# Transposing a tile's attention output with one DMA of 512 columns in place of four of 128

## The chip, the cores and the metric

One core of a Trainium2 chip (trn2). The metric is the device time of one execution in microseconds (us). The profiler's span is some 1.8 to 2.0 us shorter than that time, because it runs from the first to the last instruction alone. Each execution carries a state; all timed runs used here are of state fast. Single looks (the one profiled run, whose state is unknown) are marked as such. Three words recur. A DMA's landing is the moment when all its data have arrived. A hold is the time by which an instruction starts late because it waits for such a landing. The granted clock is the share of full speed at which TensorE was allowed to run.

## The reference, cut to what matters

Attention over 4 batches, 8 heads, 768 positions and head size 64 (three heads with the full causal mask, five with four sink positions and a window of 64), then a gated feed-forward layer on the result:

```python
scores = where(mask, q @ k.T / sqrt(64), -1e9)
attn_out = softmax(scores) @ v                                  # 4 x 8 x 768 x 64
x = attn_out.transpose(0, 2, 1, 3).reshape(3072, 512)           # a row: all 8 heads of one position
g = x @ w_gate                                                  # 512 x 1536
out = (g * sigmoid(g) * (x @ w_val)) @ w_out                    # 1536 x 512
```

## The kernel before

The 3072 rows are 24 tiles of 128. Four tiles make a group: group 3 is tiles 12 to 15, group 4 is 16 to 19, group 5 is 20 to 23. The attention of a tile ends in `xb`, 128 rows by 512 columns in fp16. The feed-forward matmuls contract over those 512 columns, so they need them on the partitions: `xt`, four blocks of 128 columns each, transposed. The order of all tasks on all engines is fixed in a list in the kernel, so no engine picks other work while it waits.

```python
def norm(t, odd):                        # VectorE: writes half of xb
    if t not in xbs:
        xbs[t] = buf("xb", [128, 4, 2, 64], FH, "xb")          # ring of 3
    ...

def xtranspose(t):
    xb = xbs.pop(t)
    g, n = GROUP[t]
    if g not in xts:
        xts[g] = buf("xt", [128, 4, 512], FH, "xt")            # ring of 2
    if t >= XBAR:                        # XBAR = 12: the later twelve tiles, by DMA
        for p in range(4):
            nc.sync.dma_start_transpose(
                out=xts[g][:, p, n * 128:(n + 1) * 128],
                in_=xb[:, p].rearrange("p a d -> p (a d)"))
        return
    tr = buf("tr", [128, 4, 128], FH, "xtr")                   # the first twelve, by TensorE
    for p in range(4):
        nc.tensor.transpose(tr[:, p, :], xb[:, p].rearrange("p a d -> p (a d)"), ident)
    trs[t] = tr

def xevac(t):                            # VectorE: the first twelve tiles alone
    g, n = GROUP[t]
    nc.vector.tensor_copy(out=xts[g][:, :, n * 128:(n + 1) * 128], in_=trs.pop(t))

def gate(g, j, c, wsb, d):               # the first reader of xt
    ps = d[g, j, c] = buf("gv", [128, 512], FP, "gv")[:, 0:c[1] - c[0]]
    for kk in range(4):
        nc.tensor.matmul(ps, wsb[:, kk, j * 128:(j + 1) * 128], xts[g][:, kk, c[0]:c[1]],
                         start=(kk == 0), stop=(kk == 3))

def store(g, tt):                        # on the same sync queue as the transposes
    ...
    for j in range(2):
        eng = nc.scalar if j and final else nc.sync
        eng.dma_start(out=rows[j], in_=o_sb[j * 64:(j + 1) * 64, :])
```

The sync engine's queue (SP) issues, in the list's order, all loads, all transposes by DMA, and the stores. An issue that has to wait holds up everything behind it (from_4_to_10 below shows a load issued 7.7 us later for that).

The softmax here doesn't subtract the row's maximum and nothing guards it: scores larger than these inputs give would overflow.

## Time and profile before

| | before |
|---|---|
| time, median of 3 runs | 271.9 us (271.53 to 271.96) |
| span of the profiled run | 269.9 us |
| TensorE busy over the span; from 128 to 227 us | 96%; 99.00 of 99.00 us |
| transposes by DMA | 48, first issue at 129.3 us, last at 222.9 us |
| share of the 16 DMA engines, 128 to 227 us | 0.20 |

How to read it: the share over the span mixes a start in which loads and casts set the pace with a long stretch in which TensorE has no gap. The transposes by DMA all lie in that stretch.

### The profile page before, as it was taken

Reading aid. Unit: us, or ns where it says so; the run is one execution under the profiler, and the core shown is the slowest. Engines: PE = TensorE matmul, PEld = TensorE weight load, DVE = VectorE, ACT = ScalarE, POOL = GpSimd, SP = SyncE. Lnnn points to the kernel's source line nnn. Section 1 sums busy time; section 2 is a strip of 40 time slices with the busy share of each in tenths; the row PEclk is TensorE's granted clock in tenths of the full one; section 3 lists DMA queues with packets and bytes.
Section 4 is the critical chain, followed back from the end, with each engine's and each line's share of the span. In section 5 each row is a group of like instructions: output and inputs, shape, how many; then the busy total and the mean of one; then the engine's idle time right before and its main releaser. Section 6 shows DMA issues by size and latency. Waiting matters only on the chain.

```text
span 269.9 us, 5396 instructions
## 1 busy us (share of the span) xinstructions
PE 258.0 (96%) x2063; PEld 150.4 (56%) x2063; DVE 173.6 (64%) x340; ACT 167.0 (62%) x260; POOL 113.1 (42%) x145
## 2 busy tenths in 40 slices
PE   7799889899999999999999999999999999999993
PEld 7777546465655565465556655555555544444441
DVE  6757787896679487657668257764582565555321
ACT  2499779999897568777657964495564603141300
POOL 6669936774786541875523223366320200000000
PEclk9999999999999999999999999999999999999998
DMA  7999999999940999011012411202002312110144
GB/s 191 294 347 350 332 282 357 341 290 294 288 150 14 257 311 275 3 40 41 19 27 58 92 40 26 56 19 62 1 15 61 89 24 51 39 40 0 41 102 92
DMA packets 56954, 36.53 MB, mean 135 GB/s; under 512 B 9312, under 2 KB 52320, under 8 KB 56928
## 3 DMA queue, kind: packets, MB, share of 16 engines
q1 hardware_dynamic: 56848, 36.06, 50.4%
q8 instruction: 16, 0.26, 0.4%
q10 hardware_dynamic: 80, 0.13, 0.2%
q14 instruction: 10, 0.08, 0.1%
HBM read 28.31 MB, written 6.29 MB: 128 GB/s over the span
## 4 chain that ended last, share of the span: by engine, by line
PE 80%; ACT 12%; DVE 5%; issue 2%; ACTq 0%
PE gv L762 42%; PE o_ps L791 21%; PE sc L524 9%; PE av L557 5%; ACT e L540 4%; PE tr L413 3%; ACT v L178 2%; ACT hq L178 2%; ACT sig L768 1%; ACT vt L178 1%; DVE m L264 1%; PE xtr L583 1%; DVE v L290 1%; DVE k L289 1%; DVE wg_sb L180 1%
## 5 line engine op out<-in xcount | busy, mean ns | idle before, releaser
L540 ACT ACTIVATE e<-sc 128x1024 f16<-128x1024 f32 (+4 forms) x67 | 60.9, 909 | 22.9 <-PE sc L524 22.5
L762 PE MATMUL gv<-xt,wg_sb 128*128 128x512 f16 (+1 forms) x304 | 71.9, 368 | 1.7 <-DVE wg_sb L180 1.1
L762 PE MATMUL gv<-xt,wv_sb 128*128 128x512 f16 (+1 forms) x304 | 72.3, 368 | 0.0
L548 POOL TENSOR_TENSOR e<-e,m 128x640 f16<-128x640 f16 (+1 forms) x25 | 44.5, 1787 | 65.8 <-ACT e L540 65.7
L791 PE MATMUL o_ps<-wo_sb,h 128*128 128x512 f16 x288 | 71.8, 379 | 0.3 <-ACT o_sb L178 0.3
L768 ACT ACTIVATE sig<-gv 128x512 f32<-128x512 f32 (+1 forms) x76 | 43.1, 575 | 44.7 <-PE gv L762 42.9
L772 DVE SCALAR_TENSOR_TENSOR sil<-sig,gv 128x512 f32<-128x512 f32 (+1 forms) x76 | 49.5, 656 | 31.8 <-ACT sig L768 31.2
L779 DVE SCALAR_TENSOR_TENSOR h<-sil,gv 128x512 f16<-128x512 f32 (+1 forms) x76 | 48.8, 654 | 9.6 <-PE gv L762 8.5
L762 PEld LDWEIGHTS <-wg_sb 128*128 128x128 f16 x304 | 28.9, 98 | 29.3 <-DVE wg_sb L180 1.4
L762 PEld LDWEIGHTS <-wv_sb 128*128 128x128 f16 x304 | 28.8, 98 | 26.5 <-issue 0.2
L791 PEld LDWEIGHTS <-h 128*128 128x128 f16 x288 | 26.6, 98 | 26.4 <-issue 0.7
L524 PE MATMUL sc<-qT,kT 128*128 128x256 f16 (+1 forms) x228 | 35.2, 257 | 1.4 <-ACT e L540 0.8
L180 POOL COPY v<-vt 32x528 f16<-32x528 f16 (+1 forms) x46 | 29.4, 640 | 6.4 <-ACT vt L178 3.7
L524 PEld LDWEIGHTS <-kT 128*128 128x128 f16 x228 | 20.6, 98 | 13.3 <-issue 2.7
L180 POOL CAST vt<-raw 64x512 f16<-64x512 f32 x30 | 18.7, 625 | 16.2 <-DMA raw<-in_v_dram 11.3
L557 PEld LDWEIGHTS <-e 128*128 128x128 f16 x472 | 20.1, 97 | 7.5 <-issue 0.5
L565 DVE RECIPROCAL rc<-av 128x4 f32<-128x4 f32 x48 | 8.6, 180 | 24.1 <-PE av L557 23.7
L178 ACT CAST hq<-raw 128x512 f16<-128x512 f32 x32 | 19.3, 617 | 4.2 <-DMA raw<-in_q_dram 2.9
L557 PE MATMUL av<-vt,e 128*128 128x65 f16 x392 | 21.7, 193 | 0.2 <-DVE xb L566 0.2
L566 DVE TENSOR_TENSOR xb<-av,rc 128x256 f16<-128x256 f32 x48 | 20.4, 424 | 1.7
L413 PE MATMUL tr<-ident,hq 128*128 128x128 f16 x192 | 15.0, 219 | 2.1 <-DVE m L264 1.1
L413 PEld LDWEIGHTS <-hq 128*128 128x128 f16 x192 | 12.2, 98 | 5.6 <-DVE m L264 1.2
(57 smaller groups left out, 192.1 us busy)
## 6 DMA issues: line engine op xcount, KB each, us to landing
raw<-in_q_dram SPq DMA_DIRECT2D x12, 512.0 KB, 7.2
raw<-in_k_dram SPq DMA_DIRECT2D x12, 512.0 KB, 7.0
raw<-in_v_dram SPq DMA_DIRECT2D x12, 512.0 KB, 7.5
out_dram<-o_sb SPq DMA_DIRECT2D x47, 128.0 KB, 2.3
raw<-in_moe_w_gate_dram SPq DMA_DIRECT2D x6, 512.0 KB, 8.7
raw<-in_moe_w_val_dram SPq DMA_DIRECT2D x6, 512.0 KB, 8.7
raw<-in_moe_w_out_dram SPq DMA_DIRECT2D x6, 512.0 KB, 7.6
xt<-xb SPq DMA_TRANSPOSE x48, 2.3
```

The source lines that it names most:

```text
L178: nc.scalar.copy(out=dst, in_=src)
L180: ENG[task.way[0]].tensor_copy(out=dst, in_=src)
L413: nc.tensor.transpose(tr[:, p, :, j, :] if w else tr[:, j, p, :], hqs[n][:, w, j, p // 2, (p % 2) * 128:(p % 2 + 1) * 128], ident)
L524: nc.tensor.matmul(sc[c // 4][:, c % 4:c % 4 + n, :], weights, moving, start=first, stop=last)
L540: nc.scalar.activation(out=e[:, 0:n], in_=whole_sc.pop((t, u))[:, 0:n], func=AF.Exp, scale=scale)
L548: ENG[task().way[0]].tensor_tensor(out=ev, in0=ev, in1=mm, op=ALU.mult)
L557: nc.tensor.matmul(av[:, n, 0:65], ee, vv, start=(m == 0), stop=(m == len(bl) - 1))
L762: nc.tensor.matmul(ps, wsb[:, kk, j * 128:(j + 1) * 128], xt[:, kk, c[0]:c[1]], start=(kk == 0), stop=(kk == 3))
L768: nc.scalar.activation(out=sg[g, j, c], in_=gs[g, j, c], func=AF.Tanh, scale=0.5)
L772: nc.vector.scalar_tensor_tensor(out=sl[g, j, c], in0=sg.pop((g, j, c)), scalar=1.0, op0=ALU.add, in1=gs.pop((g, j, c)), op1=ALU.mult)
L779: nc.vector.scalar_tensor_tensor(out=hs[g, j][:, c[0]:c[1]], in0=sl.pop((g, j, c)), scalar=0.5, op0=ALU.mult, in1=vs.pop((g, j, c)), op1=A ...
L791: nc.tensor.matmul(o_open[g, tt], hs[g, j][:, tt * 128:(tt + 1) * 128], wo_sb[:, j, :], start=(j == 0), stop=(j == NJ - 1))
```

## The change

The intent: one instruction for a tile in place of four. It saves 36 of 48 issues on the sync queue and should bring each tile's transposed block sooner.

```diff
         if t >= XBAR:
-            for p in range(4):
-                nc.sync.dma_start_transpose(
-                    out=xts[g][:, p, n * 128:(n + 1) * 128],
-                    in_=xb[:, p].rearrange("p a d -> p (a d)"))
+            nc.sync.dma_start_transpose(
+                out=xts[g][:, :, n * 128:(n + 1) * 128],
+                in_=xb.rearrange("p a b d -> p (a b d)"))
             return
```

## The prediction

> **What bounds the kernel now.** I read four views, in this order: the engines' shares and the chain of waits on the profile's page, busy time by stretch, the waits of TensorE, and then the timeline of the queue that issues the transposes (SP, the sync engine) beside TensorE's.
>
> The page first:
>
> ```profile
> PE 258.0 (96%) x2063; PEld 150.4 (56%) x2063; DVE 173.6 (64%) x340; ACT 167.0 (62%) x260; POOL 113.1 (42%) x145
> PE 80%; ACT 12%; DVE 5%; issue 2%; ACTq 0%
> xt<-xb SPq DMA_TRANSPOSE x48, 2.3
> ```
>
> TensorE is busy for 258.0 of 269.9 us, and 80% of the chain that ended last is TensorE. No DMA is among the engines of that chain. The last line is what the change touches: 48 transposes, four for each of tiles 12 to 23, each landing a median 2.3 us after its issue.
>
> An average hides stages, so next the busy time by stretch (columns: stretch, length, TensorE busy with its matmul count, granted clock, mean share of the 16 DMA engines, GB/s):
>
> ```profile
> 0.00:70.00 70.00, 62.76 (x678) 1.00 1.09 307
> 70.00:128.00 58.00, 58.00 (x457) 1.00 0.57 148
> 128.00:227.00 99.00, 99.00 (x755) 1.00 0.20 44
> 227.00:270.00 43.00, 38.26 (x178) 0.97 0.21 49
> ```
>
> The idle of TensorE lies before 70 us, where loads, casts and masks set the pace, and in the last few microseconds. The transposes run from 129.3 us (the first starts there) to about 226 us. In just that stretch TensorE is busy for 99.00 of 99.00 us at full clock, and the DMA engines are at 0.20.
>
> Busy time is modelled from pipelined matmuls, so I did not stop there. The waits of TensorE over the whole run name warm-up, masks, weight casts, exps and evictions, the largest 1.4 us; none is a DMA. Restricted to 120 to 265 us the list is empty. Short holds can be too small for that list, so I looked at the three places where TensorE first needs a group's transposed activations. Tiles 12-23 form groups 3, 4 and 5 of four tiles each; the first gate matmul of group 3 is number 161 of the 304 that read wg_sb (64 of group 0, then 48 for each group), of group 4 number 209, of group 5 number 257. Those stand at 151.83, 187.87 and 225.26 us:
>
> ```profile
> 151.83 1.11 PE L762 MATMUL gv<-xt,wg_sb 128*128 128x512 f16 x4
> 155.80 1.89 PE L762 MATMUL gv<-xt,wg_sb 128*128 128x512 f16 x8
> 187.87 1.03 PE L762 MATMUL gv<-xt,wg_sb 128*128 128x512 f16 x4
> 225.26 2.01 PE L762 MATMUL gv<-xt,wg_sb 128*128 128x512 f16 x8
> ```
>
> And the last four transposes of each group on the queue (start, time from first to last issue):
>
> ```profile
> 146.34 5.02 SPq L577 DMA_TRANSPOSE xt<-xb  x4
> 181.24 4.92 SPq L577 DMA_TRANSPOSE xt<-xb  x4
> 219.09 5.00 SPq L577 DMA_TRANSPOSE xt<-xb  x4
> ```
>
> The reader sees how tight the schedule is. Group 3's fourth transpose is issued at 150.13 and lands 2.4 us later, at 152.5, while its first gate matmul starts at 151.83: it already runs, because the first of its four matmuls needs only the first of the four 128-column pieces. Group 4's last lands at 187.3 (184.93 + 2.4), 0.55 us ahead of 187.87. Group 5's last lands at 225.9 (222.85 + 3.1), behind 225.26. So two starts should show a hold, and they do: four matmuls take 1.11 us in place of 1.03 (the undisturbed four at 187.87), eight take 2.01 in place of 1.89 (the undisturbed eight at 155.80). The holds are 0.08 and 0.12 us. **That is all the time that TensorE gives to these transposes: 0.20 us.**
>
> **What the Trainium skill says.** "VectorE: DVE Perf Modes", section "The three transpose paths", gives 1309 ns for a 128x128 transpose through the DMA crossbar. The trace's issue on the queue has a median of 1.23 us (48 instructions), near that; to landing it is 2.3 us. "DMA: Bandwidth & Descriptors", section "Rules for kernel authors", says to join many small transfers into a large one, since under 64 KB one pays mostly overhead. The trace agrees: one piece is 32 KB (128 x 128 x 2 B), and over 130 to 145 us, with only transposes in flight, the share of the DMA engines is 0.12, so a transpose keeps them busy for about 0.15 us (0.12 x 15 us / 12) out of 2.3. The same page, section "Latency and other measured facts", has 261 GB/s for DMA transposes that are not contiguous; 32 KB at that rate is 0.13 us, and my 0.15 fits. "Perfetto Trace Analysis", section "Optimization Strategies", says to optimize what the matmul engine waits for when it idles; here it doesn't idle, so that advice doesn't point at the transposes.
>
> **The change, part by part.**
> - Removed: 36 of 48 issues on the SP queue. Four back to back take 5.0 us.
> - Added: the remaining 12 are four times as large, 128 KB. If the overhead is per instruction, the issue stays near 1.2 to 1.7 us, and landing is 2.3 + 3 x 0.15 = about 2.8 us. Both are estimates from the numbers above. The queue is freed by about 12 x (5.0 - 1.5) = 42 us; nothing but stores follows on it in this stretch.
> - Moved: a tile's transposed block is complete about 2.8 us after the first issue in place of 6.2 (146.34 to 152.5), some 3.4 us earlier. For the first matmul of a group the wait becomes one for the whole block in place of one piece after another, but the block would be there at about 149.1, 184.0 and 221.9 us, ahead of 151.83, 187.87 and 225.26 by 2.7 to 3.9 us.
> - Moved: stores issued behind transposes go out up to 3.5 us sooner, so output buffers come free sooner.
> - Unchanged: TensorE's instructions and their order (fixed in a list), the first 129 us, and the end, where TensorE works through the last output products and the final eviction and store follow.
>
> Sum on the path: minus 0.08 minus 0.12 us; the other 42 us lie beside TensorE's work. An earlier store relieves no hold that TensorE shows in this stretch, so it counts as 0. 271.9 - 0.2 = **271.7 us**.
>
> **The rivals.**
> 1. The latency of the transposes is on the path. Then 3.4 us would come off at each group boundary, 10 us in all, and the time would be about 261.7. For it: landing and use lie within a microsecond of each other at all three boundaries. Against it, decisively: the matmuls start on time but for 0.20 us, other matmuls having been placed ahead of them.
> 2. The wide transpose costs the same as four (cost per 128 columns, not per instruction). Then the block lands when the fourth piece did, but the first matmul waits for all of it: group 3 starts at 152.5 in place of 151.83, group 5 at 225.9 in place of 225.26, some 0.7 us each where 0.2 in all was lost: about +1.2, so 273.1 us. If even the landing time of 2.3 us scaled by four (9.2 us), the three starts would slip to 155.5, 190.4 and 228.3, by 3.7, 2.5 and 3.0 us: about 281 us, 3.3% slower. Against it: the engines are busy for 0.15 us of 2.3, and most of the rest should not grow with size. What no line shows is how this chip handles a source of four column groups in one instruction.
> 3. The sooner stores free output buffers and help the evictions. For it: VectorE waits 2.1 us once for a store to land. Against it: TensorE's waits on evictions after 120 us are none, so at most a tenth or two, inside the range.
>
> **Range and chances.** The change's own effect is 0 to -0.2 us in the main case, up to +1.2 in the milder form of rival 2, which I give one in ten. The three runs before spread over 0.43 us. I choose 271.1 to 272.4: the predicted value with that spread on both sides, a little more above for rival 2. Faster by over 2% would need 5.4 us and TensorE has no such idle time in the stretch: 0.01. Slower by over 2% needs the strong form of rival 2 or something unseen: 0.02. Within 2%: 0.97.
>
> **What would show each step right or wrong.** Right: 12 transposes, each issued in under 2 us and landing in under 3.5; TensorE busy in all of 128 to 227 us; first gate matmuls of the three groups at nearly the same times with four in 1.03 and eight in 1.89; fewer waits in the SP queue behind transposes and earlier stores. Rival 2: issue of about 5 us each, landing in 6 or more, and a TensorE wait on xt at one of the boundaries. Rival 1: the chain from 128 us on shorter by microseconds. The prediction is wrong if the time leaves 271.1 to 272.4, above all if TensorE's matmuls between 128 and 227 us move by more than half a microsecond.

## The result, and the profile after

The changed kernel is correct. Its median is 271.43 us (271.0 to 271.52, 4 runs), against 271.74 us (271.53 to 271.96, 4 runs) of the kernel before. The ratio is 0.9985, with a 95% interval of 0.9968 to 1.0003: the same at 2%, and even no difference at all lies inside. (A ratio is the mean time of one kernel's fast runs over that of the other's in the same rounds, so not quite the ratio of the medians quoted.)

The page of the kernel after: the engines' shares, the chain by engine, and the row of the transposes (count, median us from issue to landing).

```profile
PE 257.9 (96%) x2063; PEld 150.2 (56%) x2063; DVE 173.6 (64%) x340; ACT 167.1 (62%) x260; POOL 113.0 (42%) x145
PE 80%; ACT 12%; DVE 5%; issue 2%; ACTq 0%
xt<-xb SPq DMA_TRANSPOSE x12, 2.4
```

Four times the data, and 2.4 us to landing where it was 2.3. The engines' busy times and the chain are what they were. The queue in the timeline of the kernel after (start, time from first to last issue, count):

```profile
129.31 12.32 SPq L576 DMA_TRANSPOSE xt<-xb  x3
...
143.66 1.20 SPq L576 DMA_TRANSPOSE xt<-xb  x1
...
181.21 1.19 SPq L576 DMA_TRANSPOSE xt<-xb  x1
...
213.93 5.59 SPq L576 DMA_TRANSPOSE xt<-xb  x2
```

Tile 15, the last of group 3, is now issued at 143.66 us in place of 146.34, and takes 1.20 us of the queue in place of 5.02. The queue had been backlogged there: the twelve narrow issues for tiles 12 to 14 had held it with hardly a break from 129.26 to 144.97 us. And TensorE at the three places where a group's transposed block is first read:

```profile
151.88 1.03 PE L761 MATMUL gv<-xt,wg_sb 128*128 128x512 f16 x4
187.84 1.03 PE L761 MATMUL gv<-xt,wg_sb 128*128 128x512 f16 x4
225.23 1.89 PE L761 MATMUL gv<-xt,wg_sb 128*128 128x512 f16 x8
```

Both holds are gone: four matmuls in 1.03 us where they took 1.11, eight in 1.89 where they took 2.01. TensorE starts the three groups when it did before, within 0.05 us, because its other work keeps it busy until then.

The time of a whole run is too noisy for 0.2 us, but the trace is not. Take two fixed instructions, the first gate matmul of group 2 (the 113th that reads wg_sb) and the last output matmul, and look at the distance between their starts (from the trace's start times in ns; the views round to 0.01 us):

| profiled run | first gate of group 2, us | distance to the last output matmul, us |
|---|---|---|
| before | 108.16 | 156.726 |
| after | 108.21 | 156.520 |
| after, again (wide_again) | 108.24 | 156.520 |
| after, a third time (wide_third) | 108.17 | 156.519 |

The distance of the changed kernel repeats to 0.001 us, and the change takes **0.206 us** off it: 0.083 between the starts of groups 3 and 4, 0.121 between the start of group 5 and the end, and 0.002 elsewhere. The kernel before was traced once. Most of what varies from run to run lies before 108 us: in the ten runs in which nothing before that point was altered, group 2 starts between 107.84 and 108.26 us.

### The profile page after: what moved, and what is told of

It reads as the page before. It is cut to its first block, busy times and chain, and to the rows that moved or that the text cites. A ratio compares the mean times of both kernels' runs of the same rounds, so it can differ in the third digit from the quotient of the medians.

```text
span 269.7 us, 5353 instructions
## 1 busy us (share of the span) xinstructions
PE 257.9 (96%) x2063; PEld 150.2 (56%) x2063; DVE 173.6 (64%) x340; ACT 167.1 (62%) x260; POOL 113.0 (42%) x145
## 4 chain that ended last, share of the span: by engine, by line
PE 80%; ACT 12%; DVE 5%; issue 2%; ACTq 0%
PE gv L761 42%; PE o_ps L790 21%; PE sc L524 9%; PE av L557 5%; ACT e L540 4%; PE tr L413 3%; ACT v L178 2%; ACT hq L178 2%; ACT sig L767 1%; ACT vt L178 1%; DVE m L264 1%; PE xtr L582 1%; DVE v L290 1%; DVE k L289 1%; DVE wg_sb L180 1%
```

## The experiments

Theory: TensorE is the bound from 70 us on; the transposes cost it two short holds and nothing else. Rivals: the effect is more than the holds (earlier stores, a freed queue); the latency of the transposes is on the path; the wide form costs what four narrow ones cost.

### wide_again: the changed kernel in more rounds

The edit: none.

> The changed kernel unaltered, timed in more rounds. Theory (TensorE bounds everything from 70 us on, and the change only takes away the two holds of 0.09 and 0.13 us at the starts of groups 3 and 5): 0.2 us less than the kernel before, ratio 0.999. Rival (earlier stores or fewer issues on the sync queue help beyond that): 0.4 us or more, ratio 0.9985 or lower, with TensorE idle before 120 us or after 227 us lower than before.

Measured: median 271.5 us (5 runs), before 271.61 us (9 runs), ratio 0.9994, interval 0.9981 to 1.0008. The theory's 0.999 is inside and the rival's 0.9985 too, so the timing does not decide. The distance in the table above does: 0.206 us after 108 us, the size of the two holds. Ahead of 108 us the two kernels issue the same instructions.

### last_wide and last_narrow: which transposes carry it

```diff
-            nc.sync.dma_start_transpose(            # one, 512 columns
-                out=xts[g][:, :, ...], in_=xb...)
+            if t in (15, 23):                       # last_wide; last_narrow: t not in (15, 23)
+                <the wide form>
+            else:
+                <the four narrow ones>
```

> Wide transpose for tiles 15 and 23 alone (the last of groups 3 and 5), four narrow ones for the other ten. Theory: these two carry the whole effect: both holds gone, spans within 0.1 us of the changed kernel's, although the queue still spends 50 us on narrow transposes. Group 3's block issued at about 146.3 us, because the queue is still backlogged, lands at about 148.8 us. Rival (gain comes from freeing the queue as a whole): the holds remain or the span stays at the kernel before's 269.9 us.

> The converse: wide for ten tiles, four narrow ones for tiles 15 and 23. Theory: group 3's hold goes all the same, because it came from the backlog of the queue: tile 15's first issue moves from 146.3 to about 143.7 us, its last piece lands at about 149.8 us, before 151.8. Group 5's issue starts at about 218.3 us with no backlog, its last piece lands at 224.5 to 225.2 us, so a hold of 0 to 0.05 us. Rival (a hold is set by the 6.2 us of the narrow form itself): both holds stay near 0.09 and 0.13 us.

Measured (one look each; both correct): 271.38 us and 271.33 us. Distance from group 2's first gate to the last output matmul: 156.519 and 156.523 us. Both carry the whole effect of the change. The last issues of groups 3 and 5, and TensorE's first reads, in the timelines of last_narrow:

```profile
143.29 4.95 SPq L582 DMA_TRANSPOSE xt<-xb  x4
217.96 4.95 SPq L582 DMA_TRANSPOSE xt<-xb  x4
151.51 1.03 PE L767 MATMUL gv<-xt,wg_sb 128*128 128x512 f16 x4
224.86 1.89 PE L767 MATMUL gv<-xt,wg_sb 128*128 128x512 f16 x8
```

With tiles 15 and 23 still narrow (4.95 us each), there is no hold (1.03 and 1.89 us). What caused the two holds was therefore not the narrow form of those two tiles in itself but that they were issued late, behind the narrow transposes of the tiles before them: at 146.34 and 219.09 us before, at 143.29 and 217.96 here. (Group 5's margin is small even so: the fourth piece landed at 225.35 us, and the fourth of the first matmuls was due at 224.86 + 3 x 0.216 = 225.5.)

Group 5's hold had a second cause, which the prediction overlooked. In the kernel before, the matmul that was held is the third: its piece, issued at 221.58 us, landed after 4.2 us in place of the usual 2.33, at 225.78, when that matmul was due at 225.69. A 16 KB DMA of the kind "instruction" was in flight meanwhile (queue q8, from 223.72 to 224.68 us). The queue's timeline at 222 us, and the DMA view from 221.58 to 225.78 us:

```profile
221.58 1.23 SPq L577 DMA_TRANSPOSE xt<-xb  x1
q8 instruction: 1, 0.02, 1.4%
```

Over all traces, 47 of the 52 transposes of `xb` that took over 2.7 us to land had such a DMA in flight, and only 7 of the 252 others, so it is the likely reason, though no run removed it. By this sum, with the usual landing group 5 would have had no hold in spite of the late issue (222.85 + 2.33 = 225.18 us for the fourth piece, due at 225.91). In last_narrow the fourth piece met one too (3.67 us to landing) and still came in time.

Either remedy is enough alone: shorten the last tile's transposes, or clear the queue ahead of them. The expectation for last_wide (issue at 146.3, landing at 148.8) came out as 146.73 and 149.16.

### three_dummies: give the saved time back

```diff
+            for _ in range(3):
+                spare = pools["raw"].tile([128, 4, 512], FH, name="spare", tag="raw")
+                nc.sync.dma_start_transpose(
+                    out=spare[:, :, 0:128], in_=xb.rearrange("p a b d -> p (a b d)"))
             nc.sync.dma_start_transpose(
                 out=xts[g][:, :, n * 128:(n + 1) * 128], ...
```

> Ahead of every wide transpose three more of the same size into scratch that nothing reads, so that a tile's block lands when the four narrow ones landed (about 6.2 us after the first issue) and the sync queue is as busy as before. Theory: back to the kernel before, with the wait now for the whole block: tile 15 lands at about 152.5 us, 0.7 us after the first gate matmul is due; group 4 and group 5 lose 0 to 0.2 us; in sum 0.4 to 0.9 us over the changed kernel, ratio to the kernel before 1.001 to 1.003. Rival (latency of the transposes is on the path): 3 times 3.7 us, over 10 us more than the changed kernel.

Measured: 273.89 us (4 runs), ratio to before 1.0082 (1.0068 to 1.0096). The distance is 159.189 us, 2.67 more than the changed kernel's. The mechanism is the theory's (a wait for the whole block at group 3, a smaller one at group 5), but the size is three times the upper end of what I expected. The waits of TensorE from 120 us on, and the timelines at group 3:

```profile
PE gv L765 <- DMA xt<-xb: 2.0, 1, 2.0
```

```profile
147.51 3.87 SPq L578 DMA_TRANSPOSE spare<-xb  x3
151.42 1.26 SPq L580 DMA_TRANSPOSE xt<-xb  x1
...
153.98 1.04 PE L765 MATMUL gv<-xt,wg_sb 128*128 128x512 f16 x4 [2.00 <-DMA xt<-xb]
```

I had taken tile 15's first issue from the kernel before (146.3 us). Here it comes at 147.51, because the twelve issues for tiles 12 to 14 last until 146.14 us in place of 144.97 (one of them took 2.46 us); the four issues of tile 15 follow one another at 1.3 us, the block lands at 153.93, and the matmul starts at 153.98, some 2.2 us late. Group 5 holds for 0.47 us. So a queue as busy as before cost time only at the two boundaries where a block landed later than TensorE needed it. The rival's 10 us is refuted.

### late_23 and late_23_five: how much slack one boundary has

```diff
+            for _ in range(7 if t == 23 else 0):    # late_23; late_23_five: 5
+                <a wide transpose into scratch>
```

> Seven scratch transposes ahead of tile 23's wide one alone, so its block comes about 8.7 us later (first issue 218.3, 8 issues of 1.25 us, landing 2.4 us after the last: about 229.5 us) where the first gate matmul of group 5 is due at 225.1 us. Theory: about 4.4 us of slack are used up first, and the other 4.3 us appear in full: 275.7 us (275 to 276.5), with one TensorE wait on xt at about 225 us. Rival 1 (latency on the path): 8.7 us more, 280. Rival 2 (other work of TensorE fills the gap, or later slack takes it back): under 1 us more.

> Five scratch transposes ahead of tile 23's wide one, in place of seven, which cost a hold of 4.79 us and then some 1.7 us more because eight or so matmuls of 512 columns after it ran at half rate (0.43 us apart in place of 0.215). Theory (the slack is about 4.5 us, the hold grows by 1.28 us an issue, and the half rate follows only a hold that is long): hold of about 2.2 us, no slow matmuls after it, 273.6 us (273.2 to 274.1). Rival (any hold brings a slow restart): 1 to 1.7 us more, 274.6 to 275.3.

Measured: late_23 277.94 us (277.03 to 278.98, 4 runs), 1.4 us above the upper end of my range. late_23_five 274.25 us, but in two clusters: 273.42 and 273.56, 274.93 and 275.18. TensorE at group 5 in late_23, and its busy time by stretch (columns as in the prediction, with weight loads, VectorE, ScalarE and GpSimd after TensorE; the clock follows them):

```profile
223.77 1.67 PE L765 MATMUL gv<-xt,wv_sb 128*128 128x512 f16 x7
230.06 3.48 PE L765 MATMUL gv<-xt,wg_sb 128*128 128x512 f16 x8 [4.62 <-DMA xt<-xb]
...
234.34 1.03 PE L765 MATMUL gv<-xt,wg_sb 128*128 128x512 f16 x4
```

```profile
225.00:230.00 5.00, 0.44 (x3) 0.00 (x0) 0.99 (x2) 0.00 (x0) 0.00 (x0) 1.00 0.49 98
230.00:234.00 4.00, 3.94 (x11) 1.50 (x12) 0.69 (x1) 1.01 (x2) 0.00 (x0) 0.57 0.30 70
234.00:240.00 6.00, 6.00 (x30) 2.70 (x29) 3.54 (x6) 1.38 (x3) 0.00 (x0) 1.00 0.19 44
```

The slack is as expected: the block comes 9.2 us later (landing at 229.93 in place of 220.74), 4.4 of it vanish and the hold is 4.79 us. But the eight matmuls after the hold take 3.48 us in place of 1.89, at a granted clock of 0.57 in that stretch, and full speed is back by 234.3 us. That is the second term that I had left out: the distance grew by 6.47 us, 4.79 of hold and 1.68 of slow matmuls. 271.5 + 6.5 = 278.0 us, and 277.94 was measured.

The Trainium skill had it: "TensorE: Matmul & The Clock Gate", section "Why this matters for your kernels", warns of idle gaps over about 3 us, after which the clock halves. late_23_five's hold of 2.2 us is below that, and I expected no slow restart after it. In its profiled run the hold was 2.16 us, and the slow matmuls followed all the same:

```profile
227.14 2.31 PE L765 MATMUL gv<-xt,wg_sb 128*128 128x512 f16 x8 [2.00 <-issue]
229.25 1.91 PE L794 MATMUL o_ps<-wo_sb,h 128*128 128x512 f16 x4
```

```profile
225.04:228.45 3.41, 1.41 (x8) 0.63 (x8) 0.69 (x1) 0.25 (x1) 0.00 (x0) 1.00 0.56 121
228.45:231.86 3.41, 3.41 (x10) 1.20 (x9) 2.04 (x3) 0.94 (x2) 0.00 (x0) 0.50 0.02 5
```

(The view names no releaser for the wait; the block had landed at 227.05 us. The idle that it counts, 2.00 us, is a little less than the hold, 2.16 us, by which the start is late.) Four output matmuls take 1.91 us in place of 1.03. The distance grew by 3.85 us, 2.16 of hold and 1.68 of slow matmuls, and the profiled run is the one of 275.18 us. The two runs at 273.42 and 273.56 are what the hold alone makes (271.4 + 2.16 = 273.56), with mean clocks of 1.000 and 0.997 against 0.993 for the two others. So a hold of 2.16 us brought the half rate in two of four runs, where late_23's longer one left all four at a clock of 0.991 or less. In three_dummies a hold of 2.2 us brought none in the profiled run:

```profile
149.59:153.00 3.41, 2.38 (x35) 1.66 (x33) 0.94 (x3) 3.33 (x5) 0.00 (x0) 1.00 0.47 96
153.00:156.42 3.42, 2.44 (x12) 1.14 (x13) 0.58 (x1) 2.81 (x5) 2.74 (x2) 1.00 0.75 168
```

The traces suggest what tips it. In all fourteen, each stretch of full clock lasts a whole number of steps of 3.413 us (from 12 to 78 of them), and the half rate in late_23 and late_23_five lasts one. Lay this grid, fixed by the clock's changes, over a trace and count TensorE's idle time in each step. The half rate begins 16 times, each time at the end of a step with 2.00 to 3.41 us idle; after no step with 1.95 us idle or less did it begin. In late_23_five the idle of the hold fell into one step (225.04 to 228.45 us, busy 1.41 of 3.41). In three_dummies the end of a step, at 153.00 us, cut it in two, 1.03 and 0.97 us. Where the grid lies differs from run to run, which fits two runs of four; and late_23's 4.62 us of idle leave some step with over 2.3 us wherever they fall. This was found after the runs, and no run set out to test it.

### widths: what a transpose costs by width

```diff
+            size = (256, 1024, 2048)[t % 3]
+            spare = pools["raw"].tile([128, 16, 128], FH, name="spare", tag="raw")
+            nc.sync.dma_start_transpose(
+                out=spare[:, 0:size // 128, :],
+                in_=wg_sb.rearrange("p a n -> p (a n)")[:, 0:size])
```

> After each real transpose one more of 256, 1024 or 2048 columns, in turn, from a weight tile into scratch that nothing reads: what an instruction costs as its width grows. Known: 128 columns issue 1.23 us and land at 2.33; 512 issue 1.20 and land at 2.41. If the cost were a fixed part and 0.03 us per 128 columns: 256 lands at 2.36, 1024 at 2.5, 2048 at 2.8 us, issues of about 1.2 us. If larger sizes hold the queue in proportion to the width: issues of 2048 columns of 2 us or more and landing at 3.5 or more. No expectation for the time of the kernel beyond plus 0 to 1 us.

Measured (one look, 271.92 us). The twelve together in the view by tile (duration in ns, min, median and max), and then by width, from the start, end and landing of each in the trace:

```profile
L581 SPq DMA_TRANSPOSE spare<-wg_sb x12: 1198/1299/1985, 130.6 to 219.5; - x12
DMA to landing us min/median/max: 2.3/3.1/4.4
```

| columns (KB) | time of the issue on the queue, us | issue to landing, us |
|---|---|---|
| 128 (32), kernel before | 1.23 (median) | 2.33 (typical) |
| 256 (64) | 1.20 to 1.24 | 2.34 to 2.42 |
| 512 (128), kernel after | 1.20 (typical) | 2.41 (typical) |
| 1024 (256) | 1.26 to 1.31 | 3.06 to 3.14 |
| 2048 (512) | 1.38 to 1.99 | 4.26 to 4.36 |

Up to 512 columns the width is nearly free: 0.08 us more for four times the data. From 1024 to 2048 columns the landing takes 1.2 us more, 0.15 us per 128 columns. That is the DMA time per 128 columns that the prediction read from the engines' share; up to 512 columns it hardly shows beside the 2.3 us that the narrowest takes. The expectation of 2.5 and 2.8 us for 1024 and 2048 columns was wrong, and the issue did not grow in proportion to the width either.

### from_8_to_10, from_8 and from_4_to_10: does TensorE's own work count

If TensorE is the bound, taking work off it must pay. Now that a transpose by DMA occupies the queue for 1.2 us alone, earlier tiles can use it too:

```diff
-        if t >= XBAR:
+        if t >= 8 and t != 11:     # from_8_to_10; from_8: t >= 8; from_4_to_10: t >= 4, not 7, 11
             nc.sync.dma_start_transpose(...)           # the wide form
     def xevac(t):
+        if <the same>:
+            return
```

> Tiles 8, 9 and 10 transposed by one wide DMA as well, in place of four TensorE transposes and a VectorE copy (tile 11, which has only about 1.5 us until its use, stays on TensorE). Theory: TensorE is the bound from 70 us on, so 12 transposes of about 0.056 us less (the step from one to the next in the trace) are 0.67 us off: ratio to the kernel before 0.996 to 0.997, against 0.999 for the changed kernel. Rival: the sync queue holds loads back at 96 to 102 us while it waits for these tiles, and the time stays or grows.

> Tiles 8 to 10 wide as well, beside the changed kernel on the same chip. Theory: less TensorE work before 108 us by 0.67 us, of which 0.24 us was handed back to a wait on a mask by GpSimd: 0.4 us faster than the changed kernel, first gate matmul of group 2 at 107.3 to 107.8 us in place of 107.9 to 108.2. Rival (the 0.5 us seen before was variation of the first 70 us from run to run): no difference from the changed kernel.

> Tile 11 too. Its block is ready to transpose at 106.6 us and would land at about 109.0, while the first gate matmul of group 2 is due at about 108 us less what was saved before it (0.9 us): so TensorE should wait for it by 1 to 2 us, and the time be 0.2 to 1 us above the run with tiles 8 to 10. Rival (the queue has slack here as well): a further 0.2 us faster than that run.

> Tiles 4, 5, 6 as well (all but 7 and 11 from tile 4 on), in the stretch before 70 us where TensorE is not the bound and the sync queue still issues loads one after another. Theory: no gain from TensorE's 0.67 us there, and loads that stand behind a transpose's wait come later: same as or slower than the run with tiles 8 to 10 by 0 to 2 us. Rival (the queue has room there too, and VectorE's three copies of 0.42 us were on the path): up to 1 us faster.

| run | median, us | before beside it, us | ratio (95%) | group 2's first gate, us |
|---|---|---|---|---|
| from_8_to_10 | 271.05 | 271.53 | 0.9979 (0.9967 to 0.9992) | 107.20 |
| from_8 | 272.4 | 271.53 | 1.0031 (1.0014 to 1.0049) | 108.83 |
| wide_third | 271.39 | 271.85 | 0.9981 (0.9969 to 0.9993) | 108.17 |
| from_8_to_10_again | 271.74 | 271.85 | 0.9993 (0.9980 to 1.0006) | 107.56 |
| from_4_to_10 | 273.11 | 271.85 | 1.0044 (1.0029 to 1.0058) | 109.75 |

In the profile, tiles 8 to 10 by DMA do what the theory says: group 2 starts at 107.20 and 107.56 us, ahead of all ten runs with the unaltered start (107.84 to 108.26), and the distance to the end stays 156.52 us. A part is handed back at 98.5 us, where TensorE, now ahead, waits 0.24 us (0.10 in the second run) for GpSimd's mask. The document's own measure settles the size. From group 1's first gate (the 65th matmul that reads wg_sb) to group 2's it is 34.73 us in all ten unaltered runs (34.728 to 34.734), and 34.310 and 34.173 us here: 0.42 and 0.56 us less, which is the 0.67 expected less the 0.24 and 0.10 handed back.

In the timed runs the gain does not stand: the repeat beside the changed kernel came out 0.35 us above it (expected: 0.4 below), while the run before, on another chip, suggested 0.4 below. The two profiled executions were the fastest of their five and six. What the others lost they must have lost outside the stretch that the traces show to repeat, above all before 73 us; no trace shows it. So no version here is shown to beat the changed kernel in time. wide_third was the changed kernel once more, expected 0 to 0.4 us under the kernel before; by the medians it came out 0.46 under.

from_8 shows the other side. The waits of TensorE from 95 us on:

```profile
PE gv L764 <- DMA xt<-xb: 1.4, 1, 1.4
```

Tile 11's transpose has no slack: issued at 105.96, it lands when TensorE has already stood still, and the 0.2 us saved on four TensorE transposes cost a hold of 1.58 us. That is within the 1 to 2 us expected, but the time came out 1.35 us above from_8_to_10, more than the 0.2 to 1 expected. from_4_to_10 puts transposes among the loads. The queue in its timeline:

```profile
42.21 3.75 SPq L327 DMA_DIRECT2D raw<-in_moe_w_out_dram  x2
51.73 1.87 SPq L577 DMA_TRANSPOSE xt<-xb  x1
53.71 0.51 SPq L322 DMA_DIRECT2D raw<-in_k_dram  x1
54.31 0.53 SPq L322 DMA_DIRECT2D raw<-in_v_dram  x1
```

The queue stands from 46 to 51.7 us until tile 4's attention is done. The load of k that the changed kernel issues at 46.04 us comes at 53.71, the one of v at 54.31 in place of 46.89, and group 2 starts 1.6 us later. The time is 1.4 us above the repeat with tiles 8 to 10, within the 0 to 2 expected.

## Why the prediction was right

- **TensorE bounds the stretch of the transposes.** Right. It was busy for 99.00 of 99.00 us before and after, and the distance between fixed matmuls in it stays within 156.515 to 156.523 us in every run but the kernel before and the three in which a hold was put in.
- **The transposes cost TensorE 0.08 and 0.12 us.** Right: the distance shrank by 0.206 us, and the whole of it is at groups 3 and 5. The predicted 271.7 us against 271.43 measured is a difference within what the start of the run varies; the time alone, with no difference inside its interval, would have confirmed nothing. One reading was incomplete: the prediction puts group 5's hold down to the last piece, but the matmul held was the third, and its piece was late by a slow landing (4.2 us, see last_narrow). That this fell at a boundary in the profiled run is in part luck.
- **The wide form's cost.** Right in the issue (1.20 us; estimated 1.2 to 1.7) and that it is per instruction; mis-sized in the landing: 2.41 us where 2.8 was estimated. The term "3 x 0.15" was added to the landing time of the narrow form; the runs showed 0.08 in its place. It had no weight, since the slack was 2.7 us or more by the prediction and 4.2 or more as measured. (The 0.13 us that the prediction works out for 32 KB from the 261 GB/s that it cites is an estimate; its own 0.15 us is 218 GB/s, close to the 217 that widths gives.)
- **When the blocks are there.** I had 149.1, 184.0 and 221.9 us; they landed at 146.1, 183.7 and 220.7. For groups 3 and 5 I kept the issue times of the kernel before, though the queue behind shorter transposes moves up too; by last_narrow, that moving up is enough to remove both holds.
- **Rival 1 (latency on the path, 261.7 us)** is refuted: the last blocks of the three groups landed 3.7 to 6.4 us sooner and TensorE started the groups within 0.05 us of when it had. late_23 shows the same from the other side: of 9.2 us of delay, 4.4 vanished.
- **Rival 2 (wide costs as much as four)** is refuted by the landing of 2.4 us. What its mild form would have cost I underestimated: three_dummies, with nearly the timing that this rival supposes (group 3's block at 153.93 us where the rival has 152.5), was 2.5 us over the kernel before by distance (159.189 less 156.726), where I had put 1.2.
- **Rival 3 (earlier stores help)**: some stores did go out earlier (those behind tile 15 at 144.96 us in place of 151.46), but VectorE's one wait for a store stayed (2.1 us before, 2.2 after), and the two holds account for 0.204 of the 0.206 us.

## What to carry to other kernels

Before shortening a transfer, look for the instruction of the bounding engine that first reads what it brings, and compare its start with the landing: where that engine has other work until then, the most that the change can give is the hold at those few instructions, here 0.2 us, while the queue spent 44 us less on issuing transposes (60.6 us summed over the 48 issues before, 16.5 over the 12 after). Where whole-run times are too noisy for such an effect, measure the distance between two fixed instructions of the bounding engine in the trace. The wide form is still worth having for the slack it gives a shared queue. But in these runs a transpose placed among loads, or with under 2.4 us to its first use, cost more than it saved.

## What the Trainium skill lacked or had wrong

- "TensorE: Matmul & The Clock Gate", section "Why this matters for your kernels", puts the limit for idle gaps at about 3 us. A hold of 4.79 us agrees (half rate for 3.41 us after it). But after a hold of 2.16 us the profiled run had the half rate too (granted clock 0.50 from 228.45 to 231.86 us, 1.68 us lost), and by its time one other of the four runs, while a hold of 2.2 us in three_dummies had none. The section gives one idle window as the reason. In these traces a step of 3.41 us with 2.00 us idle was enough, and one with 1.95 was not; so whether a hold of 2.2 us brought the half rate turned on where a step ended.
- "DMA: Bandwidth & Descriptors", section "DMA Transpose (X-bar)", gives no duration by width. Measured from SBUF to SBUF, 128 rows in fp16: landing after 2.33, 2.4, 2.4, 3.1 and 4.3 us for 128, 256, 512, 1024 and 2048 columns, with an issue of 1.2 to 1.3 us up to 1024. So a 128x512 transpose costs nearly the same as a 128x128 one. The step from 1024 to 2048 columns (256 KB in 1.21 us, one look) is about 217 GB/s, below the 261 and 350 to 400 GB/s that the same page's section "Latency and other measured facts" has.
- "VectorE: DVE Perf Modes", section "The three transpose paths", has 1309 ns for the DMA crossbar. Here that is near the time of the issue on the queue (1.23 us); a reader has to wait 2.3 us for the landing.
- No page was found that says what a DMA of instructions does to other transfers: 47 of the 52 transposes that took over 2.7 us to land had one in flight (4.2 us in place of 2.33 at group 5).
